# Weight chunks 12-13 ahead of a batch's last k and v, that v in two halves, larger products of M, and the scaling of two units at once

## Chip, cores and metric

The kernel runs on one core of a Trainium2 chip. The metric is device time in microseconds (us) of one execution. Times are medians of several executions, and one trace was taken for each kernel.

## The reference

Inputs are q, k, v of shape (8 batches, 8 heads, 576 positions, 64) in fp32, and two weight matrices, 512 x 2048 and 2048 x 512.

```
q_s = softmax of q over the head dimension (64)
k_s = softmax of k over the positions (576)
kv  = einsum('bhsd,bhse->bhde', k_s, v)         # 64 x 64 for each head
x   = einsum('bhsd,bhde->bhse', q_s, kv)        # attention output
x   = x, heads merged: 4608 tokens x 512
h   = x @ w_in                                  # first layer, 2048 wide
g   = h if h > 0 else exp(min(h, 0)) - 1
out = g @ w_out                                 # second layer
```

## The kernel before

A list scheduler in Python orders the instructions of each engine from modelled durations. TensorE's order is the program order. Tokens go through the two layers in nine blocks of 512. One batch is 576 tokens and two "units" of four heads each. Batch 1 is units 2 and 3, and its tokens are needed by block 1's first layer. So the attention of batch 1 is threaded into block 0's second layer, of which W2's 16 chunks of 128 rows are being loaded at the same time.

```python
W2CUT = (0, 4, 8, 12, 14, 16)            # chunks 0-3, 4-7, 8-11, 12-13, 14-15

# the loads of the prologue, in order, on the GpSimd queue
for what in (0, "2q", "3q", 1, 2, "2k", "2v", "3k", "3v", 3, 4):   # numbers: W2 pieces
    ...

# cast of v to bf16, one instruction a unit (VectorE for batch 1)
VB[:, :, :, 0:D] <- raw[:, :, :, :]      # 128 x 1152

def kv(self, units, ps, key):
    # 72 small matmuls: exp(k).T @ [v, 1]; column D gives the key sums
    ...
    for x, n in enumerate(units):        # per unit
        rz = reciprocal(PV[:, :, o + D:o + D + 1])
        for h in range(2):
            M[...] = PV[hs, :, o:o + D] * rz     # 64 x 128

def split(b):                            # the 9 columns of tokens of a batch in two pieces
    if b == 0: return 8
    left = SLOTS - b * CH % SLOTS
    return left if left < CH else 5      # batch 1: 5 and 4, so 320 and 256 tokens

# block 0's second layer: 20 pieces (4 token tiles x 5 cuts of W2); after piece number:
work = dict(zip((6, 9, 11, 14, 15, 16, 17), (
    lambda: self.tp(2, C, key), lambda: self.tp(3, Dd, key), lambda: kv([2, 3]),
    ao(2, 0, Dd), ao(2, 1, C), lambda: self.ao(3, 0, Dd, key, evac="split"), last)))
```

`tp` transposes q of a unit, `kv` makes M, and `ao` multiplies transposed q by M and evicts the result to XT, the input of the first layer. Pieces 0 to 11 use chunks 0-11 with four matmuls each. Pieces 12 to 19 have two matmuls each.

The softmax here doesn't subtract the row's maximum and nothing guards it: scores larger than these inputs give would overflow.

## Time and profile before

| | before |
|---|---|
| median | 298.96 us (4 executions, 298.74 to 299.13) |
| TensorE busy | 98% of the span |
| TensorE's waits in all | 3.2 us, of which 2.7 in the warm start |
| the wait the change aims at | 0.5 us, ahead of the k.v products of units 2 and 3 |

The head of the page of the kernel before:

```profile
span 296.8 us, 4560 instructions
...
PE 289.9 (98%) x1924; PEld 234.9 (79%) x1924; DVE 152.2 (51%) x186; ACT 153.9 (52%) x183; POOL 123.5 (42%) x131
```

The kernel is bound by TensorE, so only time that TensorE spends waiting, or on more work, can count. This view lists for whom TensorE waited (total us, times, longest us):

```profile
PE PS L464 <- DVE VB L420: 0.5, 1, 0.5
```

Line 464 is k.v, which waits for the cast of v (line 420). The next view is the chain of work that ended last, in order of time (start, length, what):

```profile
20.06 21.47 DMA VR<-in_v_dram
41.53 0.02 issue
41.55 0.78 DVE VB L420
42.33 0.04 issue
42.37 0.78 PE PS L464 x67
43.15 1.58 PE PS L672 x6
44.74 0.30 PE PS L556 x2
...
48.10 14.53 PE PS L623 x64
```

Read it from the top. The chain does not run through TensorE until 42.37 us. Ahead of that it is a DMA, the load of unit 3's v, which lands at 41.53, and its cast. From 42.37 on it is TensorE, without a break, to the end.

VectorE's groups, by shape (count, busy us, mean ns, idle before):

```profile
L482 DVE TENSOR_TENSOR MBLK<-PS,RZK 64x128 fp32r<-64x128 f32 x28 | 8.1, 289 | 1.0
L420 DVE CAST VB<-VR 128x1152 bf16<-128x1152 f32 x2 | 1.5, 766 | 2.5 <-DMA VR<-in_v_dram 2.5
```

### The profile page before, as it was taken

The numbers are of one execution on the slowest core, as the hardware profiler recorded it, in microseconds if no ns is written. First come the engines' busy times: TensorE is split into PE (matmuls) and PEld (weight loads), VectorE is DVE, ScalarE is ACT, GpSimd is POOL, SyncE is SP. The second block draws the span as 40 slices with busy tenths as digits, with TensorE's granted clock in tenths as the row PEclk, the third lists the DMA queues.
The fourth block names the chain that finished last, engine by engine and source line by source line (L and its number), as shares of the span: only waits on it lengthen the run. The fifth ranks groups of instructions, "written<-read, shape, count | busy, mean of one in ns | idle before, by whom it ended". The sixth has DMA issues, their size and how long they took to land.

```text
span 296.8 us, 4560 instructions
## 1 busy us (share of the span) xinstructions
PE 289.9 (98%) x1924; PEld 234.9 (79%) x1924; DVE 152.2 (51%) x186; ACT 153.9 (52%) x183; POOL 123.5 (42%) x131
## 2 busy tenths in 40 slices
PE   7899999999999999999999999999999999999995
PEld 2588878888888888888888888888888888888883
DVE  5857951978347913783268516760662056106600
ACT  4666358953776365546554745555534354125411
POOL 8997201753187045713472338314640055005500
PEclk9999999999999999999999999999999999999999
DMA  7999989916991697049902990089003110230022
GB/s 240 326 390 389 390 278 320 394 67 160 304 247 70 211 350 141 0 131 366 203 2 49 387 259 6 6 263 273 1 0 73 42 31 2 54 76 11 2 71 71
DMA packets 36485, 49.40 MB, mean 166 GB/s; under 512 B 16624, under 2 KB 17136, under 8 KB 36464
## 3 DMA queue, kind: packets, MB, share of 16 engines
q1 hardware_dynamic: 29792, 34.29, 39.9%
q0 software_dynamic: 6288, 14.29, 15.7%
q10 hardware_dynamic: 384, 0.53, 0.5%
q8 instruction: 15, 0.25, 0.4%
q14 instruction: 6, 0.05, 0.1%
HBM read 36.70 MB, written 9.44 MB: 155 GB/s over the span
## 4 chain that ended last, share of the span: by engine, by line
PE 85%; DMA 7%; POOL 6%; issue 0%; DVE 0%; ACT 0%; POOLq 0%
PE PS L672 41%; PE PS L623 39%; DMA VR<-in_v_dram 7%; POOL W L330 3%; PE PS L556 3%; PE PS L464 2%; POOL W L341 1%; POOL KR L307 1%; POOL QR L307 0%; POOL QR L724 0%; POOL VR L307 0%; DVE VB L420 0%; ACT OSB L686 0%; POOL ID L701 0%; POOLq L701 0%
## 5 line engine op out<-in xcount | busy, mean ns | idle before, releaser
L655 DVE SCALAR_TENSOR_TENSOR GT<-ESB,PS 128x1024 fp32r<-128x1024 f32 x69 | 84.1, 1220 | 113.0 <-POOL ESB L652 113.0
L672 PE MATMUL PS<-W,GT 128*128 128x512 f32 x576 | 140.0, 392 | 0.0
L623 PE MATMUL PS<-XT,W 128*128 128x512 f32 x576 | 132.6, 389 | 0.1
L623 PEld LDWEIGHTS PS<-XT,W 128*128 128x128 f32 x576 | 108.0, 188 | 22.6 <-DVE RZK L516 0.2
L672 PEld LDWEIGHTS PS<-W,GT 128*128 128x128 f32 x576 | 106.1, 188 | 20.6
L652 POOL TENSOR_SCALAR ESB<-ESB 128x1024 f32<-128x1024 f32 x69 | 72.1, 1045 | 101.4 <-ACT ESB L640 101.3
L640 ACT ACTIVATE ESB<-PS 128x1024 f32<-128x1024 f32 x72 | 73.9, 1028 | 51.2 <-PE PS L623 51.2
L686 ACT ACTIVATE OSB<-PS 128x512 f32<-128x512 f32 x36 | 21.3, 601 | 60.2 <-PE PS L672 60.0
L417 POOL CAST VB<-VR 128x1152 bf16<-128x1152 f32 x12 | 16.2, 1347 | 47.8 <-DMA VR<-in_v_dram 47.8
L576 ACT ACTIVATE XT<-PS 128x640 fp32r<-128x640 f32 (+3 forms) x26 | 16.9, 651 | 15.1 <-PE PS L556 15.1
L377 DVE TENSOR_REDUCE ZQ<-QR 128x18 f32<-128x1152 f32 (+1 forms) x18 | 21.8, 1212 | 2.7 <-ACT QR L371 2.6
L391 DVE TENSOR_TENSOR QS<-QR,RZQ 128x1152 f16<-128x1152 f32 x16 | 21.5, 1353 | 0.4
L371 ACT ACTIVATE QR<-QR 128x1152 f32<-128x1152 f32 (+1 forms) x18 | 18.5, 1053 | 2.4 <-DMA QR<-in_q_dram 2.4
L411 ACT ACTIVATE KR<-KR 128x1152 bf16<-128x1152 f32 x14 | 16.2, 1156 | 5.8 <-DMA KR<-in_k_dram 5.8
L404 POOL CAST qsT<-QR 128x1152 fp32r<-128x1152 f16 x12 | 13.8, 1148 | 7.0 <-DMA QR<-QS 7.0
L556 PE MATMUL PS<-qsT,MBLK 128*128 128x320 f32 (+4 forms) x60 | 13.5, 307 | 0.0
L556 PEld LDWEIGHTS PS<-qsT,MBLK 128*128 128x128 f32 x60 | 11.3, 189 | 2.6
L609 PE MATMUL PS<-IDLE 128*128 128x512 f16 x24 | 8.5, 504 | 1.7 <-DVE IDLE L704 1.5
L330 POOL DMA_DIRECT2D W<-in_moe_w_in_dram x16 | 10.0, 1366 | 0.0
L482 DVE TENSOR_TENSOR MBLK<-PS,RZK 64x128 fp32r<-64x128 f32 x28 | 8.1, 289 | 1.0
L341 POOL DMA_DIRECT2D W<-in_moe_w_out_dram x5 | 8.3, 2341 | 0.0
L609 PEld LDWEIGHTS PS<-IDLE 128*128 128x128 f16 x24 | 2.7, 121 | 6.1 <-issue 2.8
(41 smaller groups left out, 65.8 us busy)
## 6 DMA issues: line engine op xcount, KB each, us to landing
out_dram<-OSB SPq DMA_DIRECT2D x68, 128.0 KB, 2.6
QR<-in_q_dram SPq DMA_DIRECT2D x12, 576.0 KB, 8.1
KR<-in_k_dram SPq DMA_DIRECT2D x12, 576.0 KB, 5.8
VR<-in_v_dram SPq DMA_DIRECT2D x12, 576.0 KB, 6.8
W<-in_moe_w_in_dram POOLq DMA_DIRECT2D x16, 256.0 KB, 9.6
W<-in_moe_w_out_dram POOLq DMA_DIRECT2D x3, 1024.0 KB, 16.5
KR<-in_k_dram POOLq DMA_DIRECT2D x4, 576.0 KB, 13.6
QR<-in_q_dram POOLq DMA_DIRECT2D x2, 576.0 KB, 14.1
```

The costliest lines, as they stand in the source:

```text
L330: "gp", 530, lambda e, kc=kc: e.dma_start(self.W1[:, kc, sl], w[kc, :, :, sl]), key,
L371: lambda e, part=part: e.activation(part, part, AF.Exp), key,
L377: S.add("dve", 1350 if n > 1 else 750, lambda e, z=z, src=src: e.tensor_reduce(z, src, AX.X, ALU.add), key, R=self.q_res(n) if n > 1 else ...
L391: S.add("dve", 1400, lambda e: e.tensor_tensor(qso, raw[:, :, :, :], rz, ALU.mult), key, R=qR + [f"RZQ{i}"], W=[f"QS{al}"], low=True, tag= ...
L556: return e.matmul(P[:, f * 512:f * 512 + n_], M[:, f, :], T[:, c0:c1, f * 64:f * 64 + 64], start=True, stop=True)
L576: S.add("act", t_act(2 * n_, True), lambda e: e.activation(dst, src, AF.Copy), key, W=names(0) + names(1), X=self.banks(ps), tag=f"evx{n}")
L623: last = e.matmul(P[:, t * 512:(t + 1) * 512], self.W1[:, kc, tt * 128:(tt + 1) * 128], self.XT[:, kc, rc:rc + BLK], start=(kc == 0), stop ...
L640: S.add("act", t_act(1024, True), lambda e: e.activation(esb[:, :], P[:, :], AF.Exp), key, W=[f"E{i}"], X=self.banks(ps), tag=f"exp{j}.{g}")
L652: S.add("gp", 1120, lambda e: e.tensor_scalar(esb[:, :], esb[:, :], 1.0, 0.0, ALU.min, ALU.max), key, X=[f"E{i}"], tag=f"min{j}.{g}", port ...
L655: S.add("dve", t_dve(1024), lambda e: e.scalar_tensor_tensor(gt, esb[:, :], -1.0, P[:, :], ALU.add, ALU.max), key, R=[f"E{i}"], W=gw, X=se ...
L672: last = e.matmul(dst, GT[:, jj, ts * 128:(ts + 1) * 128], self.W2[:, jj, :], start=(jj == 0), stop=(jj == 15))
L686: S.add("act", t_act(512, True), lambda e: e.activation(osb[:, :], src, AF.Copy), key, W=[f"O{i}0", f"O{i}1"], X=[f"b{bk}"], tag=f"evo{jb} ...
```

## The change

The intent is to give TensorE more to do before it needs v. Chunks 12-13 are loaded ahead of unit 3's k and v, so three more pieces of the second layer can run ahead of k.v. v comes in two halves, so that the first is cast while the second is in flight. Fewer pieces are then left behind k.v. To fit, M of both units is scaled by one set of instructions, and M's products become one 448-token piece a unit (all that block 1 needs). The last 128 tokens come in four small products ahead of block 1.

```diff
-        for what in (0, "2q", "3q", 1, 2, "2k", "2v", "3k", "3v", 3, 4):
+        for what in (0, "2q", "3q", 1, 2, "2k", "2v", 3, "3k", "3v", 4):
 ...
+            elif what == "3v":
+                for h in range(2):
+                    gp = self.load_half(3, "v", h, -50, gp)
 ...
+        elif vconv == "halves":
+            for h in range(2):
+                ... tensor_copy(VB[:, h, :, 0:D], raw[:, h, :, :])     # 128 x 576
 ...                                                     # in kv(), for both units at once
+        self.RZ[:, :, :] = reciprocal(KV[:, :, :, D:D + 1])            # 128 x 4
+        for h in range(2):
+            self.MB[hs] = KV[hs, :, :, 0:D] * self.RZ[hs]              # 64 x 256
 ...
-        if b == 0:
-            return 8
+        if b < 2:
+            return 8 - b
 ...
-                    work = dict(zip((6, 9, 11, 14, 15, 16, 17), (
+                    work = dict(zip((6, 9, 14, 17, 18), (
                         lambda: self.tp(2, C, key), lambda: self.tp(3, Dd, key), lambda: kv([2, 3]),
-                        ao(2, 0, Dd), ao(2, 1, C), lambda: self.ao(3, 0, Dd, key, evac="split"), last)))
+                        lambda: self.ao(2, 0, Dd, key, evac="split"),
+                        lambda: self.ao(3, 0, C, key, evac="split"))))
 ...
+                self.ao_last(1, Dd, key)                 # four 128-column products
-            A, Bs, C, Dd = Dd, C, A, Bs
+            A, Bs, C, Dd = (Dd, C, A, Bs) if j else (C, Dd, A, Bs)
```

## The prediction

> **What bounds it now.** TensorE. The page has it busy 98% (289.9 of 296.8 us); the table by stretches has it full from 48.0 us to the end of the matmuls at 293 us. The waits by engine hold only 3.2 us of TensorE waiting, nearly all in the warm start, which the change doesn't touch. The one wait that it aims at is 0.5 us, "line 464 <- VectorE VB": unit 3's v lands at 41.53 us (the last DMA in the chain of waits), its cast takes 0.77, and TensorE, through with chunks 0-11 at 41.82, starts the k.v products of units 2 and 3 at 42.37. VectorE (51%) and ScalarE (52%) have room, so VectorE time saved is worth nothing by itself.
>
> The Trainium skill (Perfetto Trace Analysis, Identifying the Most-Contended Engine) warns that matmul busy time is no good measure of nearness to the limit. Here the chain agrees with it anyway: 64 matmuls of 512 columns take 14.51 us, 227 ns each, block after block.
>
> **What moves.**
> - Loads. Landings follow the issue order: 0.59 MB takes 1.50 us, 0.52 MB 1.34. Chunks 12-13 land near 39.9 (used from 41.8); unit 3's k slips from 40.03 to about 41.4 (with its exp of 1.16, ready at about 42.6); v's second half lands near 42.9, a half cast is about 0.45 (estimate from 0.77), so v is ready near 43.4. The last chunks land as before, 44.1, and are wanted at about 44.7.
> - TensorE order. Three pieces (six matmuls, 1.38 us) go ahead of the k.v products, reached at 43.2: the 0.5 us wait shrinks to about 0.2. k.v ends near 44.2; the three pieces before M's products take 1.4-1.6.
> - M. Two times (0.17 + 0.61) on VectorE become 0.17 + 2 x 0.42 (289 ns for 128 elements; 128 more at about 1.1 ns, from the 256- and 320-column casts of 0.42 and 0.49; an estimate). Ready near 45.4, used near 45.7: no wait, small margin. Later blocks save 0.5 us of VectorE each, off the chain.
> - M's products. The same eight weight loads and columns, as 448 + 128 instead of 320 + 256. The small ones cost about 0.1 us more together (four 64-column ones took 0.37 us).
> - Block 1's first layer now needs unit 3's 448-column eviction (ScalarE and VectorE halves, about 0.55 and 0.62) to finish behind one piece and the small products (0.46 + 0.35): even, so 0 to 0.3 us of new wait. The last 128 tokens belong to block 2; nobody waits for them.
>
> **On the critical path.** Saved: 0.3 of wait. Given back: 0.1 of small matmuls, about 0.05 of new wait. Everything after 48 us is bound by TensorE and shifts by the rest.
>
> **Predicted time** 298.85 us, range 298.40 to 299.35. Faster by over 2%: 0.01; within 2%: 0.98; slower by over 2%: 0.01.
>
> **What shows it.** TensorE's wait behind VB becomes 0.1-0.3; block 1's first layer starts at 47.6-48.1 us; the rest of the chain keeps its lengths (14.51 us a layer). M's group is 14 instructions of about 0.42 us, not 28 of 0.29. v's halves land at about 42.1 and 42.9.
>
> **What would make it wrong.** ScalarE's fixed order putting unit 3's exp late (k.v waits 0.5 or more); the one-piece eviction stuck behind an output eviction of 0.6 us (up to 0.5 us of wait ahead of block 1); small matmuls dearer than thought. Each is a fraction of a microsecond; two together give 299.5. The other way, k.v without any wait and no new one gives 298.4.

## The result, and the profile after

The changed kernel took 299.62 us (median of 4, 298.84 to 299.95), against 298.96 for the kernel before. The ratio is 1.0019, 95% interval 0.9998 to 1.0040. A ratio here is the mean time of one kernel's fast runs over that of the other's of the same rounds, so it is not quite the ratio of the medians. The median lies above the predicted range (298.40 to 299.35), and the small gain that was forecast was not there.

The head of the page of the changed kernel:

```profile
span 298.0 us, 4540 instructions
...
PE 290.8 (98%) x1924; PEld 235.1 (79%) x1924; DVE 149.9 (50%) x166; ACT 154.0 (52%) x182; POOL 122.3 (41%) x132
```

TensorE's wait for the cast of v, from the list of its waits:

```profile
PE PS L486 <- DVE VB L438: 0.7, 1, 0.7
```

Its chain of work over the same stretch (v's second half lands at 43.45 by the trace's landing records; the chain follows the first), and a place farther on:

```profile
20.72 22.02 DMA VR<-in_v_dram
42.74 0.02 issue
42.76 1.47 DVE VB L438 x2
44.24 0.04 issue
44.28 0.78 PE PS L486 x67
45.06 1.59 PE PS L695 x6
46.65 0.41 PE PS L576 x2
...
47.52 0.40 PE PS L576 x2
47.92 0.46 PE PS L695 x2
48.38 0.40 PE PS L610 x4
48.77 14.66 PE PS L646 x64
...
80.10 9.07 PE PS L646 x40
89.17 0.03 issue
89.20 5.74 PE PS L646 x24
```

VectorE's groups by shape:

```profile
L501 DVE TENSOR_TENSOR MBLK<-PS,RZK 64x256 fp32r<-64x256 f32 x14 | 5.9, 422 | 0.5
L438 DVE CAST VB<-VR 128x576 bf16<-128x576 f32 x2 | 1.5, 754 | 2.8 <-DMA VR<-in_v_dram 2.8
```

Four things stand out.

1. The wait that was to shrink did not: 0.7 us here against 0.5, although TensorE came to it with three more pieces done. (It is no clear growth either: the list has 0.8 for again and again_2, and 0.8 for before_again.)
2. A half cast of 576 elements takes 754 ns. The whole one of 1152 takes 766. Half the work takes all the time.
3. Block 1's first layer starts at 48.77, not 48.10. It takes 14.66 us and not 14.53. In the matmul starts, its second matmul comes 338 ns after the first instead of 227.
4. Block 2's first layer, from 80.10, has 0.3 us of extra gaps at 89 us (9.07 + 0.03 + 5.74 = 14.84, against 14.51).

The merged scaling came out as costed, 422 ns an instruction.

### The profile page after: what moved, and what is told of

Its sections match the earlier page's. It is cut to its first block, busy times and chain, and to the rows that moved or that the text cites. A ratio compares the mean times of both kernels' runs of the same rounds, so it can differ in the third digit from the quotient of the medians.

```text
span 298.0 us, 4540 instructions
## 1 busy us (share of the span) xinstructions
PE 290.8 (98%) x1924; PEld 235.1 (79%) x1924; DVE 149.9 (50%) x166; ACT 154.0 (52%) x182; POOL 122.3 (41%) x132
## 4 chain that ended last, share of the span: by engine, by line
PE 84%; DMA 7%; POOL 6%; DVE 0%; issue 0%; ACT 0%; POOLq 0%
PE PS L695 41%; PE PS L646 39%; DMA VR<-in_v_dram 7%; POOL W L347 3%; PE PS L576 2%; PE PS L486 2%; POOL W L358 1%; POOL KR L315 1%; POOL VR L315 1%; DVE VB L438 0%; POOL QR L315 0%; POOL QR L747 0%; ACT OSB L709 0%; PE PS L610 0%; POOL ID L724 0%
## 5 line engine op out<-in xcount | busy, mean ns | idle before, releaser
L434 POOL CAST VB<-VR 128x1152 bf16<-128x1152 f32 x12 | 14.3, 1194 | 54.3 <-DMA VR<-in_v_dram 51.7
L596 ACT ACTIVATE XT<-PS 128x640 fp32r<-128x640 f32 (+3 forms) x24 | 15.6, 651 | 12.3 <-PE PS L576 12.3
L576 PE MATMUL PS<-qsT,MBLK 128*128 128x320 f32 (+5 forms) x56 | 13.0, 313 | 0.0
L576 PEld LDWEIGHTS PS<-qsT,MBLK 128*128 128x128 f32 x56 | 10.6, 189 | 2.4
L358 POOL DMA_DIRECT2D W<-in_moe_w_out_dram x5 | 10.0, 2426 | 0.0
L486 PEld LDWEIGHTS PS<-VB,KR 64*64 64x64 bf16 x504 | 4.7, 107 | 3.2 <-DVE GT L678 1.8
```

Source lines behind the costliest of these rows:

```text
L576: return e.matmul(P[:, f * 512:f * 512 + n_], M[:, f, :], T[:, c0:c1, f * 64:f * 64 + 64], start=True, stop=True)
```

## The experiments

All 14 kernels computed the right result. Each was timed in five rounds against the kernel before, which had 11 executions in each set of runs. The sets' medians for the kernel before were 298.94, 298.76, 298.79 and 299.06.

This table holds what each trace says of the critical place. "Landed" is the 16th and last increment of the semaphore of unit 3's v. "Tail" is the start of the last matmul minus the start of k.v. Times are us from the start of the span.

| kernel | landed | k.v starts | k.v - landed | last matmul | tail |
|---|---|---|---|---|---|
| before, first trace | 41.53 | 42.37 | 0.84 | 292.79 | 250.42 |
| before_again | 41.70 | 42.54 | 0.84 | 292.96 | 250.42 |
| before_fast | 41.84 | 42.38 | 0.54 | 292.93 | 250.55 |
| before_split | 41.56 | 42.40 | 0.84 | 293.05 | 250.65 |
| before_merged | 41.93 | 43.23 | 1.30 (TensorE late) | 293.64 | 250.41 |
| changed, first trace | 43.45 | 44.28 | 0.83 | 293.93 | 249.65 |
| again | 43.35 | 44.19 | 0.84 | 293.51 | 249.32 |
| again_2 | 43.07 | 43.91 | 0.84 | 293.46 | 249.55 |
| whole_v | 43.08 | 43.92 | 0.84 | 293.60 | 249.68 |
| loads_first | 43.31 | 44.15 | 0.84 | 293.49 | 249.34 |
| fast_halves | 42.90 | 43.44 | 0.54 | 292.90 | 249.46 |
| both_first | 44.34 | 45.17 | 0.83 | 296.07 | 250.90 |
| old_order | 42.07 | 45.01 | 2.94 (chunks) | 294.32 | 249.31 |
| kv15_b | 43.41 | 43.95 | 0.54 | 293.03 | 249.08 |
| kv15_c | 43.00 | 43.54 | 0.54 | 292.60 | 249.06 |

(kv15's trace has its own stall and is told below: v landed at 42.68, k.v started at 43.22.)

The theories: the change itself costs something (theory A, in parts), or the result was chance, such as a late landing (theory B). The parts are A1, the shape of the half casts; A2, the order of loads on the SyncE queue; and A3, the small products.

### again and again_2: the changed kernel, twice more

No edit.

> The changed kernel once more, for the spread of its times and a second trace. In the first trace v's second half landed at 43.45 us (0.6 later than worked out), and a stall of 0.3 us stood in block 2's first layer at 89.2. Theory A (the change itself costs): half casts of 0.75, k.v wait 0.4 to 0.7, the stall at about 89 again, median 299.3 to 299.8, 0.4 to 0.7 over the kernel before. Theory B (chance: a late landing in some executions): v lands near 42.9 here, no stall in block 2, median within 0.2 of before.

Measured: 299.05 us (298.88 to 300.02), ratio 1.0011 (0.9998 to 1.0024). v landed at 43.35, so the landing was late again. The half casts took 0.75 and the wait was 0.8. There was no stall in block 2.

> The changed kernel a third time, to pool its times, since the control showed that a set of five or six runs of one and the same kernel can sit 0.1% off. Theory A: by the sums of the traces (landing 1.34 us later, tail shorter by 1.36 - 0.24) it is 0.2 to 0.3 us slower than the kernel before at equal lag; ratio 1.0005 to 1.0012. Rival (a real extra lag of the DMA in the changed kernel): ratio 1.0018 or more, as in the first four runs.

Measured: 299.16 us (298.85 to 299.43), ratio 1.0008 (0.9994 to 1.0022). v landed at 43.07. From the start of block 2's first layer to that of block 3's took 0.2 us longer than in again, with a gap of 338 ns at 89 us.

So the first result, 0.66 us over by medians, was a high draw of a kernel that is some 0.3 us slower (an estimate, from the sum below). Both theories hold a part: the lateness of the landing is chance, the rest is not.

### before_again: the control

No edit.

> The kernel before, once more, as the control: its trace says how far the landing of unit 3's v (41.53 us in the first trace) wanders between executions. In the five traces of the changed kernels block 1's first layer starts 5.18 to 5.21 us after that landing (4.89 with the fast half casts), in the kernel before 6.41 after it. Theory A: here too 6.4 us after whatever the landing is; ratio 1.000 within 0.001. Rival (the changed kernel lands its v late by itself): v lands at 41.5 again, within 0.1.

Measured: 299.07 us, ratio 1.0011 (0.9998 to 1.0023) against itself. Five or six executions can sit 0.1% off, so a ratio of 1.001 proves nothing here, and the traces must decide. v landed at 41.70, 0.17 later than in the first trace, and k.v came 0.84 after it.

Is the changed kernel's v later by itself? The extra transfer ahead of it is worth 1.34 us. Subtract that from each trace with the changed order (2.68 for both_first). The ten traces with the changed order, kv15's among them, then average 41.79. The six with the old order average 41.77. The spread is 41.34 to 42.07 in all. So there is no extra lag, by which is meant a landing later than the order of the loads accounts for. The lag of any one execution is chance. It is there before the two orders part: in all sixteen traces v's landing, so corrected, comes 14.36 to 14.47 us after that of W2's first piece (27.08 in the first trace before, 27.68 in the first changed one), which every kernel issues alike. The kernel before happened to be first seen near its best.

### fast_halves: the half casts in another shape

```diff
-    VB[:, h, :, 0:D], raw[:, h, :, :]
+    VB[:, h, :, 0:D].rearrange("p c (x d) -> p x c d", x=2),
+    raw[:, h, :, :].rearrange("p c (x d) -> p x c d", x=2)
```

> The same halves, but each cast walks 2 x 9 x 32 elements, so that the outermost count is even on both sides. Theory A1[...]: each cast 0.46 us in place of 0.75, k.v starts 0.3 us earlier relative to the landing of v's second half, time 0.2 to 0.3 us below the changed kernel. Rival (0.75 is a fixed cost of such a cast): still 0.75 and no change of the time.

Measured: 299.03 us, ratio 1.0003 (0.9991 to 1.0015). The casts took 463 ns on average, and k.v came 0.54 after the landing, not 0.84. VectorE's group in this trace:

```profile
L438 DVE CAST VB<-VR 128x576 bf16<-128x576 f32 x2 | 0.9, 463 | 3.1 <-DMA VR<-in_v_dram 3.1
```

The end of the chain's first part:

```profile
21.21 21.68 DMA VR<-in_v_dram
42.90 0.02 issue
42.92 0.48 DVE VB L438
43.40 0.04 issue
```

The same elements, walked as 2 x 9 x 32, cost 0.29 us less. The trace's operands show what differed. In the changed kernel the source is one run of 576 and the destination nine rows of 64 (a row is 65 long in memory, because of the column of ones). In fast_halves both sides are 2 x 9 x 32. In the whole cast they are 1152 and 18 rows of 64. The Trainium skill (VectorE: DVE Perf Modes, What auto-detection actually checks) says that a one-source operation between SBUF tensors takes its two-port mode if the outermost counts of both sides are "both even or equal". 576 and 9 are neither, 2 and 2 are, and so are 1152 and 18. The three durations agree. The "fixed cost" rival is refuted. The median does not show the 0.2 to 0.3 us that were expected: again, in the same set, has 299.05. This trace has about 0.1 us of extra gaps in block 1, and timing can't resolve the rest.

### whole_v: v in one load again

```diff
-            elif what == "3v":
-                for h in range(2):
-                    gp = self.load_half(3, "v", h, -50, gp)
-                self.k_part(n, key, "halves" if n == 3 else vconv)
+                self.k_part(n, key, vconv)
```

> The changed kernel with unit 3's v in one load and one cast. Theory A1: the halves as built are worth nothing (one whole cast 0.77 after its landing against 0.75 after the second half's), so the time is that of the changed kernel within 0.1 us. Rival (halves help, the loss is elsewhere): 0.2 to 0.4 us slower than the changed kernel.

Measured: 299.29 us, ratio 1.0016 (1.0003 to 1.0029). That is 0.24 above the changed kernel's median of the same set, so not within the 0.1 expected, but within the noise. This trace also has 0.3 us of extra gaps in block 1. It decides at k.v: k.v starts 0.84 us after the landing with one whole cast, 0.83 to 0.84 with the two halves as built. The halves were worth nothing.

### loads_first: the order of the SyncE queue

The changed kernel's schedule also put batch 2's k and v loads behind block 0's output stores. A smaller key (the scheduler's order number) puts them back.

```diff
-    loads(n + 2, "kv", key)
+    loads(n + 2, "kv", key if j else key - 2)
```

> The changed kernel, but the SyncE queue issues batch 2's k and v loads ahead of block 0's output stores again, as the kernel before did (it issued them at 45.1 to 47.2 us, the changed kernel at 50.7 to 53.1). Theory A2 (the late loads upset the GpSimd order and this leads to the 0.3 us stall in block 2): those loads land 4 us earlier, the stall at 89 is gone, 0.2 to 0.3 us below the changed kernel. Rival (the stall comes from the slow landing of batch 3's v, whatever block 0 does): the stall stays or goes independently, no change of the median.

Measured: 299.30 us, ratio 1.0012 (1.0000 to 1.0024), no gain in the median. The first of those loads was issued at 46.8 us, not 50.65, and they landed 1.5 to 2.7 us earlier than in the first changed trace, not 4. There was no stall in block 2, but "again" has none either.

What the stall waits for can be followed in the first changed trace. The matmul at 89.20 starts 0.04 us after the end of VectorE's line 678 (89.16). That waited for GpSimd's line 675, which came behind the cast of batch 3's second v (line 434), and that cast waited for its load. GpSimd and VectorE there, and the same cast in again, where nothing stalls:

```profile
85.75 1.15 POOL L434 CAST VB<-VR 128x1152 bf16<-128x1152 f32 x1 [1.58 <-DMA VR<-in_v_dram]
86.85 2.05 POOL L675 TENSOR_SCALAR ESB<-ESB 128x1024 f32<-128x1024 f32 x2
87.93 2.35 DVE L678 SCALAR_TENSOR_TENSOR GT<-ESB,PS 128x1024 fp32r<-128x1024 f32 x2 [2.51 <-POOL ESB L675]
...
85.06 1.15 POOL L434 CAST VB<-VR 128x1152 bf16<-128x1152 f32 x1 [1.03 <-DMA VR<-in_v_dram]
```

That cast starts 5.81 us after block 2's first layer in the first changed trace (which then takes 0.33 us more), 5.67 in again_2 (0.19 more), and at most 5.5 in all other traces (at most 0.04 more). So it is the landing of batch 3's v that brings the stall, as this run's rival has it. Late loads of batch 2 are not needed for a late landing there: kv15_b (5.49) and before_fast (5.19) issue them early. Why that v lands late in some executions stays open.

### before_fast: only the halves, in the fast form, on the kernel before

The halves' loads and the casts of fast_halves were added to the kernel before, and nothing else.

> The kernel before with only unit 3's v in two loads and two half casts in the fast form (2 x 9 x 32); load order, products and M as before. Theory A (the path runs through v's landing and its cast): k.v starts 0.54 us after the landing, not 0.84, time 0.3 us under the kernel before (about 298.65), so also under the changed kernel. Rival (TensorE's own work sets the time, the wait is filled anyway): no change.

Measured: 298.75 us, ratio 0.9998 (0.9986 to 1.0010). k.v came 0.54 after the landing. But the first matmul behind k.v started 75 ns later than in the kernel before. k.v was now over at about 43.1, just as chunks 12-13 landed (43.12), so the next load had become the limit. At equal landing this is 0.17 us earlier at the last matmul (0.30 less to k.v, 0.13 longer tail). The timing can't resolve that, and the expected 0.3 was not reached.

### before_split: only the 448 + 128 cut of M's products, on the kernel before

```diff
-    if b == 0:
-        return 8
+    if b < 2:
+        return 8 - b
-    work = dict(zip((6, 9, 11, 14, 15, 16, 17), (...
+    work = dict(zip((6, 9, 11, 15, 17), (... one ao for each unit; ao_last(1, Dd, key) ahead of block 1
```

> The kernel before with only M's products of batch 1 cut as in the change, one 448-token piece a unit and the four 128-column products of the last tokens ahead of block 1. Theory A3 (the small products and the slow second matmul behind them cost 0.13 + 0.11 us): 0.2 to 0.25 us over the kernel before, with a gap of about 338 ns at the second matmul of block 1's first layer, which the kernel before does not have. Rival (the prediction's 0.1): 0.1 or less, no such gap.

Measured: 299.09 us, ratio 1.0007 (0.9995 to 1.0019). The tail is 250.65 us against 250.42, so 0.23 longer, as expected in size. Of that, 0.16 is spent ahead of block 1. The expected gap of 338 ns did not show; one of 282 ns stands there, 0.06 of the rest. TensorE's timeline (start, length, what):

```profile
47.73 0.56 PE L590 MATMUL PS<-qsT,MBLK 128*128 128x128 f32 x4
48.13 1.60 PE L626 MATMUL PS<-XT,W 128*128 128x512 f32 x6
```

The four small products hold TensorE for 0.40 us (47.73 to 48.13). By columns alone, at the 227 ns of 512 columns, they would take 4 x 128 / 512 x 227 = 0.23 us. Their weight loads, and that of the matmul behind them, start 0.11 us apart in this trace, and the products follow at that pace (62, 113, 110 and 112 ns). So they likely wait for their weights, which no run tested.

### before_merged: only the scaling of two units at once

The edit is the hunk of `kv()` and its two buffers.

> The kernel before with only the key sums and M of two units scaled at once. All theories: VectorE does 14 products of 0.42 us in place of 28 of 0.29, 3 us less work, and the time stays within 0.1 us, since M is ready well before its use either way. If it moves by more, the M chain is on the path after all.

Measured: 298.96 us, ratio 1.0004 (0.9991 to 1.0017). The tail is 250.41, the same as without it: about 3 us of VectorE's work went (8.1 to 5.9 us in M's group, 2.3 to 1.2 in the reciprocals) and none of the time. TensorE was late at k.v in this trace because of a 1.7 us wait in the warm start, which was followed by 3.3 us at a granted clock of 0.50. The table marks it.

### both_first: another 0.52 MB ahead of v

```diff
-    (0, "2q", "3q", 1, 2, "2k", "2v", 3, "3k", "3v", 4)
+    (0, "2q", "3q", 1, 2, "2k", "2v", 3, 4, "3k", "3v")
```

> The changed kernel with the last chunks (14-15, another 0.52 MB) also ahead of unit 3's k and v; TensorE's order untouched. Theory A (block 1 starts a fixed 5.2 us after v's landing, so whatever is loaded ahead of v costs its full transfer time): v lands 1.34 us later, near 44.3 to 44.7, TensorE waits about 2 us ahead of k.v, time 1.3 us over the changed kernel, about 300.4. Rival (TensorE's own work sets the time): 0.4 us or less.

Measured: 300.61 us (300.18 to 302.50), ratio 1.0070 (1.0046 to 1.0095). v landed at 44.34, k.v started 0.83 after it, and TensorE waited 2.0 us for it. So what is loaded ahead of v costs its transfer time. Two of the six executions took 301.88 and 302.50 at a mean clock of 0.992 and 0.993, and the traced one is among them. Its stretches, after the span's bounds: length, then busy us (and instructions) of each engine, granted clock, DMA share, GB/s:

```profile
43.00:45.00 2.00, 0.16 (x1) 0.00 (x0) 1.34 (x2) 1.10 (x1) 0.00 (x0) 1.00 0.04 14
45.00:46.50 1.50, 1.32 (x74) 1.15 (x75) 0.57 (x3) 0.00 (x0) 0.00 (x0) 0.96 0.61 102
46.50:50.00 3.50, 3.50 (x10) 2.86 (x9) 1.20 (x3) 1.63 (x3) 0.00 (x0) 0.53 1.00 364
```

After the wait the clock was about half for 3.5 us, and most matmuls came 426 ns apart. The Trainium skill (TensorE: Matmul & The Clock Gate, What's actually happening) says that the clock halves after an idle window of about 3.4 us, in free-running windows. The trace agrees on the halving. Here a wait of 2.0 us followed by the k.v products, which are small, was enough in the traced execution, and by the mean clock in a second of the six. A wait on TensorE can thus cost twice.

### old_order: the old load order with the new order of TensorE

```diff
-    (0, "2q", "3q", 1, 2, "2k", "2v", 3, "3k", "3v", 4)
+    (0, "2q", "3q", 1, 2, "2k", "2v", "3k", "3v", 3, 4)
```

> The changed kernel with the loads in the old order (chunks 12-13 after unit 3's v), TensorE's new order kept: it must wait for chunks 12-13 ahead of the k.v products. Theory A: v lands near 41.6, chunks 12-13 near 43.0, k.v starts 1.4 us after that at about 44.4, so the time is that of the changed kernel within 0.15 us: with TensorE starved here the order of these two loads only chooses which of them it waits for. Rival (the load order is what helps or hurts): off by 0.5 us or more.

Measured: 300.01 us, ratio 1.0032 (1.0017 to 1.0047), 0.85 above again_2 of the same set by medians. The expectation was missed, and its rival held. Chunks 12-13 landed at 43.37 and k.v started at 45.01, 1.64 us after that, for six matmuls stand between. Had the same bytes ended with v, k.v would have started 0.84 after them. The mistake was to compare the sum with a k.v start from a trace with lag. The load move is needed once TensorE's order is changed.

### kv15, kv15_b, kv15_c: the same idea with TensorE later still

kv15 takes the idea one piece further. k.v comes after all four pieces of chunks 12-13, with fast half casts. Block 1's first group is done in two halves, so that unit 3's eviction hides, and the small products come behind that group.

```diff
-    work = dict(zip((6, 9, 14, 17, 18), (
+    work = dict(zip((6, 9, 15, 18, 19), (
-        if (j, g) == (0, 2):
+        if (j, g) in ((0, 2), (1, 0)):       # kc 0, 1 first, then kc 2, 3
+                if (j, g) == (1, 0):
+                    self.ao_last(1, Dd, key)
-            A, Bs, C, Dd = (Dd, C, A, Bs) if j else (C, Dd, A, Bs)
+            A, Bs, C, Dd = Dd, C, A, Bs
```

(and the edits of fast_halves and loads_first)

> An attempt to beat both: the changed kernel with fast half casts, the k.v products one piece later (after all of chunks 12-13), M's products one piece later, the first layer's first group taken as two halves (inputs of unit 2, then of unit 3) so that unit 3's eviction hides behind the first half, the small products behind that group, and the k and v loads ahead of the stores. By theory A: TensorE reaches k.v at about 43.65 with v ready at about 43.45, so no wait in an execution without lag, and 1.81 us of matmuls moved against 1.34 us of landing: 0.3 to 0.5 us under the kernel before, 298.4 to 298.7. Rival (new waits at the first group or at the small products eat it): 299 or more.

Measured: 299.99 us (298.50 to 302.23), ratio 1.0042 (1.0010 to 1.0074). A new wait stands in TensorE's list:

```profile
PE PS L576 <- POOL qsT L421: 2.3, 1, 2.3
```

The altered schedule had put unit 5's q reduction on VectorE at 61.85 us. In the kernel before, the second such reduction of that stretch ran at 55.86. Its transposed q came late, and the clock dropped to 0.61 for 4.4 us behind that wait. The rival was right for kv15 as built, though the new wait was not where it put it. Two mends followed:

```diff
-    elem_q(2, k1)                             # kv15_b
+    elem_q(2, 16)
-    loads(n + 2, "kv", key if j else key - 2) # kv15_c
+    loads(n + 2, "kv", key)
```

> kv15 with the q work of batch 2 at a slightly earlier key, which in the scheduler's own plan puts unit 5's reduction back where the kernel before has it. Theory A: no stall at 78 us; k.v without a wait or with less than 0.2; block 2's first layer about 0.4 us earlier than in the kernel before at equal landing; time 0.3 to 0.5 us under the kernel before, ratio 0.9983 to 0.9990. Rival (something else is lost): ratio 0.9995 or more with no stall in the trace.

Measured: 298.72 us (298.47 to 299.02) against 299.06 of the same set, ratio 0.9985 (0.9972 to 0.9998). Its trace has the second latest v of the nine with that order (43.41). Still the list of TensorE's waits holds none behind the cast of v, nor kv15's, and the chain now runs through TensorE ahead of k.v (line 486) too:

```profile
40.28 3.69 PE PS L695 x16
43.98 0.75 PE PS L486 x67
44.73 0.02 issue
44.74 1.66 PE PS L695 x6
```

But TensorE is not last here, only about even with v. The weight load of k.v still waited for the cast, by the view of the cast's line (who waited for it, us, times):

```profile
  PEld PS L486: 0.4, 1
```

In all three kv15 traces k.v starts 0.54 to 0.55 us after the landing, as it does in fast_halves, where TensorE plainly waits. It starts 366 to 392 ns after the matmul ahead of it, against 318 and 327 in before_merged and old_order, where the cast had long been done. So the wait left is some 0.05 us (an estimate from these numbers). And the first matmul behind k.v starts 0.04 us after the landing of the last chunks (44.70 in kv15_b): the next load is now as late as v. By the sum used below, kv15_b is 0.30 - 1.34 + (250.42 - 249.08) = 0.30 us faster than the kernel before at equal lag.

> kv15 with the k and v loads of batch 2 behind the stores, as in the changed kernel; the plan then also has unit 5's reduction in its old place. Theory A: as kv15_b, ratio 0.9983 to 0.9992, perhaps now and then a small stall near 89 us as in the changed kernel. Rival: ratio 0.9995 or more.

Measured: 298.93 us (298.38 to 299.53), ratio 0.9993 (0.9980 to 1.0007), no stall in its trace. kv15_b is faster than the kernel before by an interval that is only just clear of 1. The control sat 0.11% off, so the timing alone is no proof; the sum of the traces agrees with it. kv15_b is also below every median of the changed kernel, though those come from other sets of runs. The gain measured is 0.15%.

## Why the prediction was wrong

The prediction's central step was "the 0.5 us wait shrinks to about 0.2". The sum of the traces shows what took its place. From the kernel before to the changed one, at equal lag of the DMA:

| term | predicted | measured |
|---|---|---|
| landing of v, for 0.52 MB ahead of it | 1.34 later | 1.37 later (mean of the nine traces with 0.52 MB more ahead of v, 43.14, against 41.77 for the six without) |
| landing to k.v | 0.84 to about 0.5 | 0.84 to 0.84 |
| six matmuls off the tail | 1.38 | 6 x 0.227 = 1.36 |
| M's products and their wake | 0.1 more | 0.23 more (before_split), 0.26 by the sum (249.32 - 250.42 + 1.36) |
| scaling of M | 0 | 0 |

The sum is 1.34 + 0 - (250.42 - 249.32) = 0.24 us slower (0.27 with the 1.37 measured), and stalls in block 2 of 0 to 0.3 us come on top. The three ratios, 1.0008 to 1.0019, agree with that but could not have shown it alone.

Point by point:

- **The load move is a wash by itself; the prediction had both sides right.** It delays v by 1.34 us and takes 1.36 us of matmuls off the tail. both_first shows the first half of this, old_order and the tails the second. As long as TensorE waits at k.v, the time is v's landing plus a fixed tail. A gain must come from a shorter step between landing and k.v, or from unlocking more work than the bytes cost, as kv15_b's eight matmuls do.
- **The half cast was mis-sized: "a half cast is about 0.45 (estimate from 0.77)", measured 0.754.** This is the term that failed: with it the wait did not shrink to 0.2 us but was 0.7 to 0.8, and the 0.3 us that were to be saved between landing and k.v were not. (With the fast casts of fast_halves, at next to no lag, the wait is 0.4: TensorE came to k.v at 43.02, some 0.2 us sooner than the 43.2 worked out. That costs nothing as long as v is what it waits for.) The estimate took the whole cast's rate over to another shape, and the shape lost the fast mode. whole_v and fast_halves show it from both sides. With 0.46 the gap from landing to k.v is 0.54, which is what the prediction had counted on.
- **The products were mis-sized: "about 0.1 us", measured 0.23.** The four small ones alone take 0.40 us where their columns account for 0.23.
- **"0 to 0.3 us of new wait" ahead of block 1** came, and was small. It is not in the list of waits, but VectorE's and the weight loads' timelines of the first changed trace show it:

```profile
47.96 0.62 DVE L592 CAST XT<-PS 128x448 fp32r<-128x448 f32 x1 [0.24 <-PE PS L576]
48.63 0.53 PEld L646 LDWEIGHTS PS<-XT,W 128*128 128x128 f32 x3
```

  Unit 3's eviction ends at 48.58, and the first weight load of block 1 starts 0.05 us later, as in the other seven traces with this order of products. In before_split the eviction ends 0.43 us ahead of that weight load, and the second matmul comes 282 ns after the first, not 338. So less than 0.1 us of the wake is this wait, and the sums (0.26 against 0.23) put it at 0.03, near the 0.05 predicted.
- **A stall in block 2** came, where the prediction said that the lengths would stay. It follows a late landing of batch 3's v (see loads_first), and what makes that late stays open.
- **Chance explains the rest of the miss.** The first changed trace had v 0.58 later than the first trace before plus 1.34. Across all traces the lag has the same mean in both orders. The prediction took one trace's landing as the landing, and it was the second earliest of sixteen. By the Trainium skill (DMA: Bandwidth & Descriptors, Why a DMA increments its semaphore by 16 and not by 1), a transfer has landed only when all 16 engines have counted up. In these traces the first and the sixteenth increment of v are 1.8 us apart (before) to 2.4 us (again). Why the slowest engine lags more in some executions was not tested; the lag is there by the first landing of W2.
- **Right:** the bound, the place of the wait, M's 0.42 us, the uselessness of saved VectorE time.

## What to carry to other kernels

Before filling a wait, see what ends it. If it ends with a DMA and its cast, then bytes moved ahead of that DMA push the wait back by their transfer time, and only the work that they unlock beyond that is a gain. When an operation is cut in half, don't halve its time: look at the access patterns that it is left with, and measure. Where a gain is 0.1%, sum a path over several traces and run the unchanged kernel against itself, for a set of five executions can sit 0.1% off.

## What the Trainium skill lacked or had wrong

- VectorE: DVE Perf Modes has the rule, but doesn't say that an operand's touching rows arrive merged into one run while the other's padded rows don't, so that the source and the destination of an equal-looking copy differ in outermost count. Here 576 against 9 rows took 754 ns, 2 x 9 x 32 on both sides 463 ns, and the whole 1152 against 18 rows 766 ns.
- TensorE: Matmul & The Clock Gate gives about 3.4 us of idleness for the halving of the clock. A wait of 2.0 us, followed by 72 small k.v products, brought it in the traced execution of both_first (granted clock 0.53 for 3.5 us), and a wait of 1.7 us in the warm start of before_merged did too (0.50 for 3.3 us). The wait of about 1.3 us in old_order did not.
- TensorE: Matmul & The Clock Gate has no figure for the spacing of fp32 products of 128 columns between larger ones: here four of them held TensorE for 0.40 us, about 0.11 us each behind the first, and M's products in that cut made the tail 0.23 us longer.
- DMA: Bandwidth & Descriptors says that the 16 engines finish independently, but gives no figure for how far apart. Here the sixteenth increment of one 0.3 to 0.6 MB load came 1.8 to 2.4 us after the first, and its time wandered by 0.7 us between executions.
